# A decode block on one core: weight blocks cut by rows instead of by columns, with partial sums added outside PSUM and a new order of the late loads

## The chip, the cores and the metric

The kernel runs on one core of a Trainium2 chip. The metric is the device time of one execution in microseconds, as the median of several runs, lower being better. A ratio is the mean time of one kernel's runs over that of the kernel before in the same rounds on the same chip. It is therefore not quite the ratio of the medians that are quoted beside it.

A profile is one execution. Its span, from first to last instruction, is about 2 us shorter than the time. Positions "at 360 us" are counted from the start of the span.

## The reference, cut to what matters

One token per sequence, for 8 sequences, goes through a modulated attention and a modulated gated MLP. All tensors are bf16.

```
mod = silu(c) @ w_mod                              # w_mod 1024 x 6144
h = layernorm(x) * (1 + ca) + sa
q = h @ wq                                         # wq 1024 x 4096, 32 heads of 128
o = softmax(q @ k_cache^T / sqrt(128)) @ v_cache   # each cache 8 x 4 x 8192 x 128
x = x + ga * (o @ wo)                              # wo 4096 x 1024
h = layernorm(x) * (1 + cb) + sb
x = x + gb * ((relu(h @ W_gate) * (h @ W_up)) @ W_down)   # 1024 x 3584, 3584 x 1024
```

Each cache has 8 sequences x 4 heads x 8192 positions x 128, and a head of the cache serves 8 query heads. One sequence's head is 2 MB, so the 64 of K and V are 134 MB. The weights are 51 MB. Each byte is used once, so the work is to move 186 MB into the core.

## The kernel before: the parts that matter

Weights travel in blocks of up to 2 MB into slots of SBUF. There are four weight slots (`wslot`), four for K (`ksl`), three for V (`vsl`) and one scratch area (`scr`) that serves the MLP at the end. SP issues the weight and K loads in one fixed order, and waits in that order. ACT issues the V loads. Blocks of w_mod, wq, gate and up are cut by columns:

```python
for jb in range(6):
    wblocks.append(("mod", jb, w_mod[:, 1024 * jb:1024 * (jb + 1)].rearrange("(kc p) n -> p kc n", p=128), KC, 1024))
...
def dense_T(i, act_T, col_of_fb, nfb, key_last=None):
    pe_wait_wblock(i)
    ...
    for fb in range(nfb):
        for kc in range(KC):               # all 8 parts of the contraction are in the block
            pe.op(... e.matmul(T.X_ps[:, col:col + B], wv[:, kc, 128 * fb:128 * (fb + 1)], act_T[:, kc, :],
                               start=(kc == 0), stop=(kc == KC - 1)), ...)
```

A partition then receives eight pieces of 1,024 columns, 2,048 bytes each (1,024 bytes in the last, narrower block of gate and up). K and V give each partition one piece of 16,384 bytes. A slot is loaded again when its last reader is done. For the late weights the rule is:

```python
if region in region_last:      free = ("pe", ("wdone", region_last[region]))
elif region[0] == "w":         free = None
elif region[0] == "k":         free = ("pe", ("sdone", last_k_user[region[1]]))   # scores 28..31
elif region[0] == "v":         free = ("pe", ("pvdone", last_v_user[region[1]]))
else:                          free = ("pe", ("pvdone", B * G - 1))
```

On PE, a batch's four score products come first, and the products with V of the batch before come around the softmax steps (cut):

```python
for b in range(B):
    st_phase(b)                                 # 4 K tiles: scores
    if b >= 1: pv_pairs(b - 1, [0, 1])          # 2 V tiles of the batch before
    softmax_pe_1(b)
    if b >= 1: pv_pairs(b - 1, [2, 3])
    softmax_pe_2(b)
pv_pairs(B - 1, [0, 1]); pv_pairs(B - 1, [2, 3])
```

Then follow wo, the second norm, gate/up and down. Down's blocks go into the weight slots that wo leaves. K31 and V31 below are the last K and V tiles (counted from 0).

## Time and profile before

| | kernel before |
|---|---|
| time | 457.57 us median of 4 (457.41 to 458.21) |
| span | 455.6 us |
| bytes | 186.4 MB, mean 409 GB/s |
| PE / DVE / ACT busy | 40% / 20% / 5% |
| chain that ended last | DMA 82% |

The next fence has lines of the page: the DMA engines' mean busy share in tenths in 40 slices of the span, what they moved, packets by size, SP's load queue q1 (packets, MB, share of the 16 engines) and the chain that ended last.

```profile
...
DMA  7999999999999999999999999999999999999992
GB/s 293 443 402 408 407 407 424 432 405 424 433 434 419 432 430 433 426 429 426 434 427 427 431 432 421 430 434 429 424 432 433 416 431 421 412 365 382 379 405 94
DMA packets 35838, 186.40 MB, mean 409 GB/s; under 512 B 1464, under 2 KB 3512, under 8 KB 27600
...
q1 hardware_dynamic: 31184, 118.54, 64.1%
...
DMA 82%; PE 11%; SPq 3%; DVE 2%; issue 2%; ACT 0%
```

The DMA row is full from the second slice to the last but one, so time is bytes over rate. The rate is not the same everywhere. The windows view shows it: each line has a stretch, its length, busy time and count of PE, weight loads, DVE, ACT and GpSimd, the granted PE clock, the DMA share and GB/s.

```profile
34.00:68.00 34.00, 13.37 (x456) 12.79 (x456) 1.30 (x5) 0.00 (x0) 0.00 (x0) 1.00 1.05 408
250.00:300.00 50.00, 19.64 (x589) 17.78 (x588) 15.96 (x13) 3.82 (x2) 0.00 (x0) 1.00 1.01 430
360.00:370.00 10.00, 5.89 (x194) 5.38 (x194) 2.44 (x2) 0.00 (x0) 0.00 (x0) 1.00 1.01 413
400.00:420.00 20.00, 10.85 (x288) 9.31 (x284) 5.44 (x11) 0.20 (x1) 0.00 (x0) 0.95 1.01 368
```

With 16,384-byte packets (250 to 300 us) it is 430 GB/s. With 2,048-byte packets (34 to 68 us) it is 408, though the engines are no less busy. In the MLP's loads (400 to 420 us) it is only 368. Single packets in the trace took a median of 611 ns for 16,384 bytes, 84 for 2,048 and 46 for 1,024.

### The profile page before, as it was taken

The numbers are of one execution on the slowest core, as the hardware profiler recorded it, in microseconds if no ns is written. First come the engines' busy times: TensorE is split into PE (matmuls) and PEld (weight loads), VectorE is DVE, ScalarE is ACT, GpSimd is POOL, SyncE is SP. The second block draws the span as 40 slices with busy tenths as digits, with TensorE's granted clock in tenths as the row PEclk, the third lists the DMA queues.
The fourth block names the chain that finished last, engine by engine and source line by source line (L and its number), as shares of the span: only waits on it lengthen the run. The fifth ranks groups of instructions, "written<-read, shape, count | busy, mean of one in ns | idle before, by whom it ended". The sixth has DMA issues, their size and how long they took to land.

```text
span 455.6 us, 11881 instructions
## 1 busy us (share of the span) xinstructions
PE 183.4 (40%) x5784; PEld 170.3 (37%) x5784; DVE 90.4 (20%) x101; ACT 22.6 (5%) x17; POOL 1.3 (0%) x9
## 2 busy tenths in 40 slices
PE   2013431340362652354175245317524544373853
PEld 2013431330362652353164235316414543372853
DVE  4000100025025025004302500420250033004001
ACT  3000001001001001001000100100010011000000
POOL 1000000000000000000000000000000000000000
PEclk9999999999999999999999999999999999998555
DMA  7999999999999999999999999999999999999992
GB/s 293 443 402 408 407 407 424 432 405 424 433 434 419 432 430 433 426 429 426 434 427 427 431 432 421 430 434 429 424 432 433 416 431 421 412 365 382 379 405 94
DMA packets 35838, 186.40 MB, mean 409 GB/s; under 512 B 1464, under 2 KB 3512, under 8 KB 27600
## 3 DMA queue, kind: packets, MB, share of 16 engines
q1 hardware_dynamic: 31184, 118.54, 64.1%
q10 hardware_dynamic: 4608, 67.11, 34.6%
q8 instruction: 45, 0.74, 0.6%
q14 instruction: 1, 0.01, 0.0%
HBM read 185.63 MB, written 0.02 MB: 407 GB/s over the span
## 4 chain that ended last, share of the span: by engine, by line
DMA 82%; PE 11%; SPq 3%; DVE 2%; issue 2%; ACT 0%
DMA ksl<-in_A_k_cache_dram 60%; DMA wslot<-in_w_mod_dram 7%; DMA vsl<-in_A_v_cache_dram 7%; DMA wslot<-in_A_wq_dram 4%; DMA wslot<-in_B_W_down_dram 4%; PE S_ps L495 3%; SPq L61 3%; PE X_ps L477 3%; PE X_ps L578 2%; PE OT_ps L512 2%; PE S_ps L467 1%; DVE mpart L392 1%; DVE xc L348 0%; DVE stat L343 0%; DVE S_ps L351 0%
## 5 line engine op out<-in xcount | busy, mean ns | idle before, releaser
L512 PE MATMUL OT_ps<-scr,vsl 128*128 128x8 bf16 x2048 | 59.5, 168 | 105.7 <-DMA vsl<-in_A_v_cache_dram 105.4
L512 PEld LDWEIGHTS OT_ps<-scr,vsl 128*128 128x128 bf16 x2048 | 57.0, 104 | 107.9 <-DMA vsl<-in_A_v_cache_dram 107.4
L495 PE MATMUL S_ps<-qT,ksl 128*128 128x8 bf16 x2048 | 58.6, 168 | 66.3 <-DMA ksl<-in_A_k_cache_dram 53.6
L495 PEld LDWEIGHTS S_ps<-qT,ksl 128*128 128x128 bf16 x2048 | 56.6, 104 | 68.2 <-DMA ksl<-in_A_k_cache_dram 41.9
L392 DVE TENSOR_REDUCE mpart<-S_ps 128x32 f32<-128x2048 f32 x8 | 18.3, 2292 | 142.2 <-PE S_ps L495 142.2
L409 DVE TENSOR_REDUCE lpart<-scr 128x32 f32<-128x2048 bf16 x8 | 28.6, 3571 | 15.8 <-ACT scr L319 15.8
L319 ACT ACTIVATE scr<-scr 128x2048 bf16<-128x2048 f32 x8 | 15.3, 1909 | 285.6 <-DVE scr L404 285.6
L477 PE MATMUL X_ps<-siluT,wslot 128*128 128x8 bf16 x384 | 11.2, 168 | 35.8 <-DMA wslot<-in_w_mod_dram 35.8
L477 PEld LDWEIGHTS X_ps<-siluT,wslot 128*128 128x128 bf16 x384 | 10.7, 104 | 36.3 <-DMA wslot<-in_w_mod_dram 32.2
L404 DVE TENSOR_TENSOR scr<-S_ps,nb 128x2048 f32<-128x2048 f32 x8 | 18.3, 2291 | 0.3
L412 DVE RECIPROCAL rrow<-X_ps 1x32 f32<-1x32 f32 x8 | 2.8, 346 | 58.7 <-PE X_ps L529 58.7
L477 PE MATMUL X_ps<-hT,wslot 128*128 128x8 bf16 x256 | 7.5, 168 | 12.7 <-DMA wslot<-in_A_wq_dram 12.7
L477 PEld LDWEIGHTS X_ps<-hT,wslot 128*128 128x128 bf16 x256 | 7.2, 104 | 13.1 <-DMA wslot<-in_A_wq_dram 10.0
L379 DVE COPY modT<-X_ps 128x384 f32<-128x384 f32 x1 | 0.6, 557 | 42.3 <-PE X_ps L477 42.3
L578 PE MATMUL X_ps<-ot_sb,wslot 128*128 128x8 bf16 x256 | 7.3, 168 | 3.7 <-issue 3.0
L578 PEld LDWEIGHTS X_ps<-ot_sb,wslot 128*128 128x128 bf16 x256 | 7.1, 104 | 3.9 <-issue 3.1
L477 PE MATMUL X_ps<-h2T,ksl 128*128 128x8 bf16 x256 | 7.1, 168 | 2.2 <-issue 1.6
L477 PEld LDWEIGHTS X_ps<-h2T,ksl 128*128 128x128 bf16 x256 | 7.0, 104 | 2.4 <-issue 1.7
L524 PEld LDWEIGHTS X_ps<-diag,ones 32*128 32x128 f32 x16 | 3.9, 304 | 8.7 <-DVE diag L397 8.7
L524 PE MATMUL X_ps<-diag,ones 32*128 32x32 f32 x16 | 5.0, 405 | 5.1 <-DVE diag L397 5.1
L521 PE MATMUL X_ps<-identf,mpart 128*32 128x128 f32 x16 | 5.1, 420 | 4.8 <-DVE mpart L392 2.4
L395 DVE TENSOR_REDUCE negm<-X_ps 32x1 f32<-32x128 f32 x8 | 2.2, 279 | 22.9 <-PE X_ps L521 22.9
(73 smaller groups left out, 75.5 us busy)
## 6 DMA issues: line engine op xcount, KB each, us to landing
vsl<-in_A_v_cache_dram ACTq DMA_DIRECT2D x32, 2048.0 KB, 24.0
ksl<-in_A_k_cache_dram SPq DMA_DIRECT2D x32, 2048.0 KB, 27.2
wslot<-in_w_mod_dram SPq DMA_DIRECT2D x6, 2048.0 KB, 24.0
wslot<-in_A_wq_dram SPq DMA_DIRECT2D x4, 2048.0 KB, 18.7
wslot<-in_A_wo_dram SPq DMA_DIRECT2D x4, 2048.0 KB, 26.1
wslot<-in_B_W_down_dram SPq DMA_DIRECT2D x3, 2048.0 KB, 17.9
ksl<-in_B_W_gate_dram SPq DMA_DIRECT2D x2, 2048.0 KB, 48.7
ksl<-in_B_W_up_dram SPq DMA_DIRECT2D x2, 2048.0 KB, 35.0
```

The lines of the kernel that those rows point to most:

```text
L61: self.e.dma_start(out_ap, in_ap).then_inc(self.K.dsem[sem_name], 16)
L319: act.op(lambda e: e.activation(T.pt[:, b % 2, 0:NCOL], T.ssub[:, 0:NCOL], ACT.Exp), key=("exp", b))
L392: dve.op(lambda e: e.tensor_reduce(T.mpart[:, :], T.S_ps[:, 0:NCOL].rearrange("p (c j) -> p j c", c=NCX), AX.X, ALU.max), key=("mpart", b))
L404: dve.op(lambda e: e.tensor_tensor(out=T.ssub[:, 0:NCOL].rearrange("p (c j) -> p c j", c=NCX), in0=T.S_ps[:, 0:NCOL].rearrange("p (c j) -> ...
L409: dve.op(lambda e, b=b: e.tensor_reduce(T.lpart[:, :], T.pt[:, b % 2, 0:NCOL].rearrange("p (c j) -> p j c", c=NCX), AX.X, ALU.add), key=(" ...
L467: pe.op(lambda e, fb=fb: e.matmul(T.S_ps[0:B, 128 * fb:128 * (fb + 1)], srcT[:, fb * B:fb * B + B], T.identf[:, :], start=True, stop=True) ...
L477: pe.op(lambda e, fb=fb, kc=kc, col=col, wv=wv: e.matmul(T.X_ps[:, col:col + B], wv[:, kc, 128 * fb:128 * (fb + 1)], act_T[:, kc, :], star ...
L495: pe.op(lambda e, b=b, p=p, kv=kv, cix=cix, col=col: e.matmul(T.S_ps[:, col:col + REP], kv[:, cix, :], T.qT[:, b, REP * p:REP * (p + 1)], ...
L512: pe.op(lambda e, p=p, cix=cix, col=col, vv=vv, ptv=ptv: e.matmul(T.OT_ps[:, col:col + REP], vv[:, cix, :], ptv[:, cix, REP * p:REP * (p + ...
L521: pe.op(lambda e: e.matmul(T.X_ps[0:32, 0:128], T.mpart[:, 0:32], T.identf[:, :], start=True, stop=True), key=("P1", b))
L524: pe.op(lambda e: e.matmul(T.X_ps[:, 128:160], T.ones[0:32, 0:128], T.diag[0:32, 0:32], start=True, stop=True), key=("P2", b))
L578: pe.op(lambda e, fb=fb, hq=hq, wvs=wvs: e.matmul(T.X_ps[:, fb * B:fb * B + B], wvs[hq // 8][:, hq % 8, 128 * fb:128 * (fb + 1)], T.ot_sb[ ...
```

## The change

The intent is larger packets. Blocks of w_mod, wq, gate and up are cut by rows of the weight, so that a partition's piece is a whole row: 12,288, 8,192 and 7,168 bytes. Such a block holds only a part of the contraction, and PSUM no longer sums over blocks. DVE adds each block's partial result to an accumulator in SBUF, and two PSUM banks take turns. To find room, several small buffers share memory. The order of the late loads changes too: wo's four blocks wait for batches 0 to 3, and the K slots go to gate/up only after the third-last product with V ("the gate" below). The core of the diff:

```diff
-    for jb in range(6):
-        wblocks.append(("mod", jb, w_mod[:, 1024 * jb:1024 * (jb + 1)].rearrange("(kc p) n -> p kc n", p=128), KC, 1024))
+    for kc in range(KC):
+        wblocks.append(("mod", kc, [(lambda r: r[:, 0:6 * D], w_mod[128 * kc:128 * (kc + 1), :])]))
 ... (wq: two row groups a block; gate and up: one row group of each a block)
     for i in load_order:
         region = assign[i]
-        if region in region_last:
+        if region in region_last and region_last[region] >= n_phaseA:
             free = ("pe", ("wdone", region_last[region]))
         elif region[0] == "w":
-            free = None
+            free = ("pe", ("sdone", min(B * G - 1, _wj[0] * G + G - 1)))
+            _wj[0] += 1
         elif region[0] == "k":
-            free = ("pe", ("sdone", last_k_user[region[1]]))
+            free = ("pe", ("pvdone", B * G - 3))
 ...
+            for kc in range(KC):
+                dve.wait("pe", ("modpart", kc))
+                pb = PB[kc % 2]
+                if kc == 0:
+                    dve.op(... e.tensor_copy(modflat, pb[:, 0:48 * B]) ...)
+                else:
+                    dve.wait_self()
+                    dve.op(... e.tensor_tensor(out=modflat, in0=pb[:, 0:48 * B], in1=modflat, op=ALU.add) ...)
 ... (the same for q in 4 and gate/up in 8 parts; PE waits for the add of two blocks ago before it writes a bank)
```

## The prediction

> **What bounds the kernel now: the DMA engines.** In the page's 40 slices the DMA row reads 9 in 38 of them; the chain of waits is 82% DMA. PE is busy 40%, DVE 20%. 186.4 MB move at a mean of 409 GB/s. Where only K and V move (16,384-byte packets) the windows view gives 428 to 430 GB/s; from 34 to 68 us, where only w_mod, wq and wo move (2,048-byte packets), it gives 407 to 408; from 400 to 440 us (gate/up/down, 1,024 and 2,048-byte packets) only 359 to 396.
>
> Packets in the trace take median 0.611 us for 16,384 bytes, 0.084 for 2,048, 0.046 for 1,024. Corrected for the overlap of neighbouring packets (DMA share 1.01 and 1.05) this fits about 5.6 ns fixed plus 36.6 ps per byte on one engine. The Trainium skill, "DMA: Bandwidth & Descriptors", section "Why small descriptors are slow (HBM only)", names a fixed overhead per packet (about 3 cycles); the trace agrees in kind.
>
> **What the change does.** w_mod, wq, gate and up (35.7 MB) are cut by rows, so their packets grow from 2,048/1,024 to 12,288, 8,192 and 7,168 bytes: 18,432 packets become about 4,096. wo and down stay at 2,048. Bytes and matmuls stay. Partial sums over kc move from PSUM accumulation to DVE adds: 18 small adds or copies of 128x256 to 128x448; the 128x384 copy took 0.56 us, so about 10 us of DVE, hidden under block loads of about 4 us each; one last add per stage (0.6 us) is exposed to the chain at most. The wo loads are spread over batches 0 to 3, and gate/up loads into the K slots wait for the third-last V product.
>
> **Cost, as estimates from those durations.** 14,300 fewer packets x 5.6 ns / 16 engines = 5.0 us (cross-check: 35.7 MB at 408 instead of 429 GB/s is 4.3 us). All on the DMA path: about 2.6 us before attention, 2 us after. In the tail the trace also shows starved slices (402 to 404, 408 to 413, 426 to 433 us, at 250 to 350 GB/s), together about 2.9 us of bandwidth, where SP's issues last 4 to 6 us each. Gate/up with fewer, larger packets should remove over half of that. Against it: when K's last load lands, nothing but V25/V26 is queued; V27 is issued only about 4 us later, and the gate loads that used to fill in no longer do: a hole of about 1 us. The end of the chain after the last down block (5.6 us) and the 4 to 5 us in which the DMA engines drain unevenly stay. Attention stays at about 39 us a batch.
>
> Sum: about -4.5 -2 +1 = -5.5 us. Predicted: 452.0 us, range 447.5 to 455; faster by over 2% 0.15, within 2% 0.82, slower by over 2% 0.03.
>
> **What would show it right:** packets under 8 KB from 27,600 to about 11,200; slices before attention at 425 to 430 GB/s; first K batch complete 8 to 13 us earlier because wo no longer goes first; attention slope unchanged; wo still at about 407; tail slices at 420 or more while gate/up load; the chain still ending in a wait for down.
>
> **What would make it wrong:** a hole over 3 us where gate/up loads now start; 7,168-byte packets slower than the fit; a tail bound by PE (about 50 us after the last V); large packets removing the uneven drain, which would give over 2%.

## The result, and the profile after

| | before | changed |
|---|---|---|
| time, median | 457.65 us (12 runs, 457.22 to 458.38) | 453.53 us (9 runs, 453.06 to 454.70) |
| ratio | | 0.9909 (95% interval 0.9898 to 0.9919) |
| span | 455.6 us | 451.2 us |

The change gains 0.9%, which is inside the 2% band. The prediction was 452.0 with a range of 447.5 to 455. The same lines of the changed kernel's page:

```profile
...
DMA  7999999999999999999999999999999989999993
GB/s 309 428 431 428 424 431 430 428 422 424 428 428 425 426 426 429 421 431 430 426 417 432 433 424 430 431 430 428 428 427 431 399 338 428 420 424 425 415 406 129
DMA packets 21662, 186.40 MB, mean 413 GB/s; under 512 B 1624, under 2 KB 1624, under 8 KB 11376
...
q1 hardware_dynamic: 17008, 118.54, 62.7%
...
DMA 81%; PE 12%; DVE 3%; issue 2%; SPq 1%; ACT 0%
```

and the same windows of it:

```profile
34.00:68.00 34.00, 11.66 (x392) 11.08 (x392) 4.25 (x11) 0.00 (x0) 0.00 (x0) 1.00 1.01 427
250.00:300.00 50.00, 22.57 (x702) 20.77 (x699) 17.89 (x14) 3.82 (x2) 0.00 (x0) 1.00 1.01 430
360.00:370.00 10.00, 7.08 (x214) 6.37 (x210) 4.39 (x5) 0.00 (x0) 0.00 (x0) 1.00 0.87 331
400.00:420.00 20.00, 10.68 (x265) 8.82 (x265) 6.20 (x13) 0.20 (x1) 0.00 (x0) 1.00 1.02 425
```

SP's queue has 17,008 packets for the same 118.54 MB instead of 31,184. The stretch of w_mod and wq runs at 427 GB/s instead of 408 and that of gate/up at 425 instead of 368 (in the changed kernel V2's load overlaps the first until 39.9 us; w_mod alone, from 41 to 48 us, moves at 424 against 406 before). The K/V stretch is unchanged. One thing is worse: from 360 to 370 us the rate falls to 331 (413 before). That is the hole that the gate opens between the last K and the first gate/up load.

How the end hangs together is seen in the chain of waits in order of time (start, duration, what), here from the last V on:

```profile
379.66 14.20 DMA vsl<-in_A_v_cache_dram
393.90 1.88 PE OT_ps L525 x64
...
427.05 1.49 PE OT_ps L634 x56
...
429.69 15.99 DMA wslot<-in_B_W_down_dram
445.73 1.03 PE OT_ps L651 x32
...
```

V31 lands at 393.9 us. PE and DVE need until about 428.7 for its product (L525), wo, the norm and gate/up (L634). Then PE waits, and the last block of down lands at 445.7; from there to the end of the span are 5.5 us. So two clocks run at the end: "last landing + 5.5 us", and "last V + the work that hangs on it". Here the first ends later. The chain of the kernel before ends in the same wait:

```profile
...
383.68 14.81 DMA vsl<-in_A_v_cache_dram
...
433.08 16.98 DMA wslot<-in_B_W_down_dram
...
450.10 1.03 PE OT_ps L607 x32
...
```

Comparing landings in the two traces, the last K came at 361.5 before and 358.5 after (3.0 us gained), the last V at 398.5 and 393.9 (4.6), the last block of down at 450.1 and 445.7 (4.4).

### The profile page after: what moved, and what is told of

Its sections match the earlier page's. It is cut to its first block, busy times and chain, and to the rows that moved or that the text cites. A ratio compares the mean times of both kernels' runs of the same rounds, so it can differ in the third digit from the quotient of the medians.

```text
span 451.2 us, 11940 instructions
## 1 busy us (share of the span) xinstructions
PE 184.1 (41%) x5784; PEld 170.6 (38%) x5784; DVE 100.9 (22%) x120; ACT 22.5 (5%) x16; POOL 1.3 (0%) x9
## 3 DMA queue, kind: packets, MB, share of 16 engines
q1 hardware_dynamic: 17008, 118.54, 62.7%
## 4 chain that ended last, share of the span: by engine, by line
DMA 81%; PE 12%; DVE 3%; issue 2%; SPq 1%; ACT 0%
DMA ksl<-in_A_k_cache_dram 48%; DMA vsl<-in_A_v_cache_dram 20%; DMA wslot<-in_w_mod_dram 10%; DMA wslot<-in_B_W_down_dram 4%; PE OT_ps L525 3%; PE S_ps L508 2%; PE X_ps L612 2%; PE X_ps L634 1%; PE OT_ps L634 1%; PE S_ps L494 1%; DVE guacc L427 1%; SPq L61 1%; PE OT_ps L569 1%; DVE scr L422 1%; ACT scr L324 0%
## 5 line engine op out<-in xcount | busy, mean ns | idle before, releaser
L525 PE MATMUL OT_ps<-scr,vsl 128*128 128x8 bf16 x2048 | 60.0, 168 | 86.0 <-DMA vsl<-in_A_v_cache_dram 81.5
L525 PEld LDWEIGHTS OT_ps<-scr,vsl 128*128 128x128 bf16 x2048 | 57.2, 104 | 88.3 <-DMA vsl<-in_A_v_cache_dram 83.1
L410 DVE TENSOR_REDUCE guacc<-S_ps 128x32 f32<-128x2048 f32 x8 | 18.3, 2292 | 141.5 <-PE S_ps L508 141.5
L427 DVE TENSOR_REDUCE guacc<-scr 128x32 f32<-128x2048 bf16 x8 | 28.5, 3568 | 15.8 <-ACT scr L324 15.8
L422 DVE TENSOR_TENSOR scr<-S_ps,guacc 128x2048 f32<-128x2048 f32 x8 | 18.3, 2291 | 0.3
L569 PE MATMUL X_ps<-siluT,wslot 128*128 128x8 bf16 x192 | 5.7, 168 | 17.5 <-DMA wslot<-in_w_mod_dram 17.5
L569 PE MATMUL OT_ps<-siluT,wslot 128*128 128x8 bf16 x192 | 5.8, 168 | 16.0 <-DMA wslot<-in_w_mod_dram 16.0
L569 PEld LDWEIGHTS X_ps<-siluT,wslot 128*128 128x128 bf16 x192 | 5.4, 104 | 17.8 <-DMA wslot<-in_w_mod_dram 15.2
L569 PEld LDWEIGHTS OT_ps<-siluT,wslot 128*128 128x128 bf16 x192 | 5.4, 104 | 16.4 <-DMA wslot<-in_w_mod_dram 16.4
L537 PEld LDWEIGHTS X_ps<-guacc,ones 32*128 32x128 f32 x16 | 4.0, 304 | 8.7 <-DVE guacc L415 8.7
L537 PE MATMUL X_ps<-guacc,ones 32*128 32x32 f32 x16 | 5.0, 405 | 5.1 <-DVE guacc L415 5.1
L545 PE MATMUL X_ps<-guacc,ones 1*128 1x32 f32 x16 | 5.0, 407 | 3.5 <-DVE guacc L430 3.5
```

Source lines behind the costliest of these rows:

```text
L410: dve.op(lambda e: e.tensor_reduce(T.mpart[:, :], T.S_ps[:, 0:NCOL].rearrange("p (c j) -> p j c", c=NCX), AX.X, ALU.max), key=("mpart", b))
L422: dve.op(lambda e: e.tensor_tensor(out=T.ssub[:, 0:NCOL].rearrange("p (c j) -> p c j", c=NCX), in0=T.S_ps[:, 0:NCOL].rearrange("p (c j) -> ...
L427: dve.op(lambda e, b=b: e.tensor_reduce(T.lpart[:, :], T.pt[:, b % 2, 0:NCOL].rearrange("p (c j) -> p j c", c=NCX), AX.X, ALU.add), key=(" ...
L525: pe.op(lambda e, p=p, cix=cix, col=col, vv=vv, ptv=ptv: e.matmul(T.OT_ps[:, col:col + REP], vv[:, cix, :], ptv[:, cix, REP * p:REP * (p + ...
L537: pe.op(lambda e: e.matmul(T.X_ps[:, 128:160], T.ones[0:32, 0:128], T.diag[0:32, 0:32], start=True, stop=True), key=("P2", b))
L545: pe.op(lambda e: e.matmul(T.X_ps[:, 192:224], T.ones[0:1, 0:128], T.rrow[0:1, 0:32], start=True, stop=True), key=("P4", b))
```

## The experiments

The theory: the gain is the fixed cost of packets that no longer exist, and the hole gives a part of it back. Rivals: the new order of the loads is what gains; DMA time goes by bytes alone; the adds cost on the chain; the gate is what makes large packets pay. All kernels below gave correct results and were run four times each. Landings are those of the one profiled run, in us from the start of its span.

| run | kernel | time us | ratio to before | last V | last down |
|---|---|---|---|---|---|
| (before) | | 457.65 | 1 | 398.5 | 450.1 |
| (changed) | | 453.53 | 0.9909 | 393.9 | 445.7 |
| e1 | changed, no gate | 459.45 | 1.0036 | 405.5 | 445.6 |
| e2 | before + both orders | 457.25 | 0.9989 | 395.9 | 450.7 |
| e3 | changed, w_mod in 1,024 B | 457.09 | 0.9982 | 397.8 | 449.7 |
| e4 | changed, DVE steps doubled | 453.60 | 0.9911 | 393.6 | 445.6 |
| e5 | before + wo spread | 457.09 | 0.9978 | 398.5 | 449.6 |
| e6 | changed, one block ungated | 454.62 | 0.9927 | 398.7 | 445.6 |
| e7 | changed, down in 16,384 B | 457.37 | 0.9975 | 395.1 | 446.1 |
| e8 | changed, one V product earlier | 453.47 | 0.9912 | 393.9 | 445.7 |
| e9 | e8, gate opens earlier | 454.07 | 0.9921 | 396.6 | 445.8 |
| e10 | changed, w_mod in 2,048 B | 455.27 | 0.9946 | 396.7 | 448.6 |
| e11 | changed, scores issued three times | 490.65 | 1.0714 | 432.6 | 484.4 |
| e12 | changed, 2,560 idle waits on GpSimd | 453.92 | 0.9914 | 394.9 | 446.8 |

### e3 and e10: is it the packets?

w_mod's rows are laid into SBUF with gaps, so that a row can't be one packet. Blocks, bytes, order and the rows read from HBM stay as in the changed kernel. e3, with 512 columns a piece (e10: 1,024 columns, pitch 1,280):

```diff
-("mod", kc, [(lambda r: r[:, 0:6 * D], w_mod[128 * kc:128 * (kc + 1), :])])
+("mod", kc, [(lambda r: r[:, 0:7680].rearrange("p (j n) -> p j n", n=640)[:, :, 0:512],
+              w_mod[128 * kc:128 * (kc + 1), :].rearrange("p (j n) -> p j n", n=512))])
```

> The changed kernel with w_mod's rows laid out with gaps in SBUF, so that its packets are 1,024 bytes instead of 12,288 (12,288 packets instead of 1,024); same bytes, same blocks, same order. Theory (5.6 ns fixed per packet and engine): 11,264 x 5.6 ns / 16 = 3.9 us more, about 457.4. Rival (DMA time goes by bytes; the packets' size is a by-product): within 0.7 us of 453.5. If the cost per packet grows for small ones, more than 5 us.

> A second dose of e3: w_mod in packets of 2,048 bytes (6,144 instead of 1,024) in the changed kernel. e3 gave 3.5 us for 11,264 more packets, 5.0 ns per packet and engine; the same cost here gives 5,120 x 5.0 ns / 16 = 1.6 us more, about 455.1. If the cost sets in only below 2,048 bytes: under 0.7 us.

The page's packet line, first e3:

```profile
DMA packets 32926, 186.40 MB, mean 409 GB/s; under 512 B 1624, under 2 KB 13912, under 8 KB 23664
```

then e10:

```profile
DMA packets 26782, 186.40 MB, mean 410 GB/s; under 512 B 1624, under 2 KB 1624, under 8 KB 17520
```

With 11,264 packets more, e3 took 3.6 us more (3.5 against e4 in the same rounds), where 3.9 was expected; with 5,120 more, e10 took 1.7 us more, where 1.6 was expected. Over 16 engines that is 5.0 and 5.4 ns for each packet on one engine. The rival "bytes alone" is out. Since the rows read are as contiguous as in the changed kernel, it is the packets and not the contiguity in HBM that count.

Another rival is that SP issues such loads more slowly (its eight issues for w_mod last 41.6 us in all in e3, 31.0 in e10 and 3.3 in the changed kernel) and so leaves engines without work. In the first 5 us that may play a part: e3 and e10 moved 108 and 97 GB/s there, the changed kernel 171, which is 0.7 and 0.9 us at full rate. Later it does not: from 41 to 48 us, where w_mod alone loads, the rates are 384, 406 and 424 GB/s, with the engines never less busy in e3 and e10 (DMA share 1.09, 1.05 and 0.99). For all of w_mod's 12.58 MB these rates make 4.4 and 4.1 ns per packet, so a part of the 5 ns may be the later start.

### e2, e5 and e1: packet size against gate

e2 gives the kernel before both new orders; e5 gives it the wo order alone; e1 takes the gate from the changed kernel. Each edit is the lines of the diff above, applied or undone, for instance e1:

```diff
         elif region[0] == "k":
-            free = ("pe", ("pvdone", B * G - 3))
+            free = ("pe", ("sdone", last_k_user[region[1]]))
```

> The kernel before with everything of the change's load order but none of its packets: wo spread over batches 0 to 3, and K slots given to gate/up only after the third-last V product. Theory (the gain is packets alone): no gain; the hole costs, so 457.6 plus 2 to 3 us, about 460. Rival (the order of the loads is what gains): 453 to 456 us.

> The kernel before with the spread of the wo loads alone (small packets, K slots free after their last score). With e1 (large packets, the same freeing), e2 (small, gated) and the changed kernel (large, gated) it makes a square of packet size by gate. Theory (wo's order is worth nothing; small packets take little from V, about a tenth beside 16,384-byte packets, so the gate matters only for large ones): 457.6 plus or minus 0.7 us, last V at about 396 to 399 us, starved stretches after 400 us as before. Rival (wo's spread is a gain that e2 hid under the gate's hole): 454 to 456 us.

> The changed kernel with one undo: a K slot is given to gate/up as soon as its last K was used (scores 28 to 31), as before the change, instead of after the third-last V product. Theory (the change gains by larger packets and gives about 3 us back in a hole that the gate opens): the hole at 360 to 372 us (331 GB/s) closes, 420 GB/s or more there, time about 450.5 us against 453.5, that is 2 to 3 us less. Rival (the gate protects V, and releasing gate/up early takes bandwidth from V and so delays the chain V, wo, norm, gate/up): the last V lands 2 us or more later than 393.9 and the time is 453.5 or more.

wo is spread in all four corners of this square:

| | K slots free after their last score | gated |
|---|---|---|
| small packets | 457.09 (e5) | 457.25 (e2) |
| large packets | 459.45 (e1) | 453.53 (changed) |

Both of my expectations about the gate fell. For small packets it costs nothing clear of noise, though its hole is there, and I had expected 2 to 3 us. (wo's order alone, e5, is worth about 0.2%: 0.9978, interval 0.9963 to 0.9993.) For large packets it is worth 5.9 us, and I had expected its removal to gain; the rival written down for e1, that the gate protects V, is what came.

First e1. The window of the hole shows that it was filled:

```profile
360.00:370.00 10.00, 5.96 (x165) 5.12 (x161) 3.38 (x5) 0.00 (x0) 0.00 (x0) 1.00 1.00 421
```

and its chain shows what that did:

```profile
386.51 19.00 DMA vsl<-in_A_v_cache_dram
...
405.56 1.88 PE OT_ps L525 x64
...
439.93 2.71 issue
...
446.80 1.87 PE X_ps L651 x64
...
```

V31 landed at 405.5 instead of 393.9. The chain no longer has a wait for down: it goes without DMA from V's product to down's (L651). All of down had landed at 445.6, and the end came only at 457.4. The work after the last V took 51.9 us (457.4 - 405.5) and it set the end. (In the changed kernel the same work would end at 393.9 + 51.9 = 445.8 us, 5.4 us before its span's end.) The prediction had named this as what could make it wrong.

Why did V suffer so much more from large packets? (With small ones the gate moves V31 from 398.5 to 395.9 us, with large ones from 405.5 to 393.9.) The Trainium skill, "DMA: Bandwidth & Descriptors", section "Queues, rings and completion order", says that an engine takes turns between the queues at the granularity of packets. The trace agrees that the turns are about even: between 377 and 392 us, e1's engines started 272 packets of gate/up and 274 of V. In e5 there were 381 and 336. (A packet of the trace is one piece of a row; the page's packet is a group of some 9 to 17 descriptors. The counts show how even the turns are, not how long one is.) When turns are about even, bandwidth goes by packet size. Gate/up took 1.95 of 6.44 MB (30%) with 7,168-byte packets, and 0.78 of 6.29 MB (12%) with 2,048-byte ones. Making the weights' packets larger thus made the weights a stronger rival to V, and the gate keeps them apart.

Now e2. In the same window its hole is as deep as the changed kernel's:

```profile
360.00:370.00 10.00, 5.50 (x193) 5.37 (x194) 2.29 (x1) 0.00 (x0) 0.00 (x0) 1.00 0.78 313
400.00:420.00 20.00, 10.27 (x251) 8.43 (x248) 5.57 (x12) 0.20 (x1) 0.00 (x0) 1.00 1.06 403
```

But from 400 to 420 us it runs at 403 GB/s with the same small packets that gave 368 before. In e5, which has the same packets and the same order of wo but no gate, it is the other way round:

```profile
360.00:370.00 10.00, 6.07 (x194) 5.54 (x194) 2.29 (x1) 0.00 (x0) 0.00 (x0) 1.00 1.04 425
400.00:420.00 20.00, 11.28 (x288) 9.43 (x285) 5.07 (x9) 0.18 (x1) 0.00 (x0) 0.99 1.00 366
```

So the hole and the low rate of the old tail, which the prediction counted as two terms, trade against each other. The landings say how. Each load raises its semaphore, the counter that its readers wait for, in 16 steps, and the trace has 16 DMA engines; I take each step as the landing of one engine's part. These are the times of the 16 parts after the first of them:

```
before,  V25 (last part at 364.6): 0.0 0.2 0.2 0.2 0.3 0.4 0.4 1.2   6.0 6.1 6.1 6.1 6.2 6.3 6.6 7.3
changed, V25 (last part at 362.3): 0.0 0.0 0.1 0.3 0.4 0.6 0.7 1.0   5.8 5.8 5.9 5.9 6.0 6.2 6.2 7.3
changed, V28 (last part at 377.4): 0.0 0.0 0.2 0.4 0.8 0.9 0.9 1.0   1.1 1.1 1.3 1.4 1.4 2.2 2.2 2.4
```

During attention eight parts come to trail the other eight by some 6 us. A load counts as landed when its last part has. In the hole of the changed kernel the early engines run dry while the late ones still have work: V25 to V30 land at 362.3, 367.1, 372.4, 377.4, 382.3 and 387.1, about 5 us apart, which is the time of 2 MB at full rate. The late engines never stop, and the hole costs those that were ahead. A count of the packets that are under way at once bears this out. From 360.5 to 363 us the changed kernel has 8 or 9, half of the usual 16, and after 363.7 never under 13 until 440 us. e2 has 7 to 9 from 363 to 365.8 us and never under 15 from 400 to 440. The kernel before and e5 have never under 15 from 355 to 400 us, and fall to 9 or 10 in short stretches after 400. So it is half of the engines that stand still, in the hole with the gate and in the tail without it. That they are the same ones from load to load is an inference, since the trace does not name the engine of a packet.

### e6, e8 and e9: is the hole worth filling?

e6 releases only the first gate/up block early (region 0 of the K slots as in e1, the rest gated). e8 leaves the loads alone and moves one product of PE, so that V24's slot is free earlier:

```diff
-                st_phase(b)
+                last_b = (b == B - 1)
+                st_phase(b, (lambda: pv_pairs(B - 2, [0])) if last_b else None)   # called before the last K's scores
                 if b >= 1:
-                    pv_pairs(b - 1, [0, 1])
+                    pv_pairs(b - 1, [1] if last_b else [0, 1])
```

e9 is e8 with the gate at `B * G - 4`.

> The changed kernel with only the first gate/up block (1.8 MB, 4.3 us of transfer) let into its K slot as soon as that slot's last score is done; the other blocks stay gated. If the hole at 360 to 372 us is time that any load could use: 2 to 3 us less than 453.5, last V delayed by under 2 us. If the hole is only where engines that run ahead wait for those that lag (paid once, here or at the end): within 0.8 us of 453.5, with the last V 2 to 4 us later. If V's chain is what ends last after all: more than 454.5.

> The changed kernel with one product moved in PE's order: in the last batch the product with V24 comes before the last K's scores instead of after them, so V24's slot is free, and V27 is asked for, some 5 us earlier (357 instead of 362 us). Nothing is added ahead of V on the DMA. If the hole at 360 to 372 us comes from V27 and V28 being asked for late: the hole shrinks to under 1 us, the last V lands 2 to 4 us before 393.9, and the time falls 2 to 3 us, to about 451. If the hole is only engines that run ahead waiting for those that lag: under 0.7 us of change.

> As e8, and the gate of gate/up opens one V product earlier (the fourth-last). If a stretch of idle DMA remains in e8 while softmax of the last batch runs: up to 1 us less than e8. If gate/up then shares with the last V loads and V's chain is near the bound: 0 to 2 us more than e8.

e6 took 454.62 us, with V31 4.8 us later (398.7), so that the work after V set the end again (452.8 - 398.7 = 54.1 us), while the last landing stayed at 445.6. e8 took 453.47 us, no change, with V31 at 393.9; its window at 360 to 370 us:

```profile
360.00:370.00 10.00, 6.60 (x192) 5.83 (x189) 4.72 (x5) 0.00 (x0) 0.00 (x0) 1.00 0.90 351
```

The hole did not close: the next request still had to wait for V25's late parts. e9 took 454.07, 0.6 more than e8, with intervals that overlap (0.9903 to 0.9940, 0.9894 to 0.9930). In e1, e4, e6, e8 and e9 the last landing is within 445.6 and 445.8 us, hole or no hole. With small packets throughout (before, e2, e5) it is 449.6 to 450.7. For e8 this is the outcome that was expected if the hole is only engines ahead waiting for those behind. e6's last landing says the same, while its time was set by the other clock.

### e4: do the adds cost?

Ahead of each partial sum's add stands a copy of the same bank (two copies of 224 columns for gate/up). That makes 28 further steps, not the 20 that the expectation says, and 12.2 us more of DVE. For instance:

```diff
                 pb = PB[kc % 2]
+                dve.wait_self()
+                dve.op(lambda e, pb=pb: e.tensor_copy(T.guacc[:, 0:48 * B], pb[:, 0:48 * B]))
                 if kc == 0:
```

> The changed kernel with a further DVE copy of each partial-sum bank ahead of its add (20 more steps on 128x224 to 128x384, about 10 us more DVE work). Theory (the adds hide under the block loads, and behind the K loads where they end a stage): under 0.7 us more. Rival (they sit on the chain): each block's add delays the next block, 5 us or more.

It took 453.60 us against 453.53. In the window from 34 to 68 us DVE was busy for 7.66 us instead of 4.25, and the rate stayed:

```profile
34.00:68.00 34.00, 11.65 (x392) 11.07 (x392) 7.66 (x18) 0.00 (x0) 0.00 (x0) 1.00 1.01 428
```

The adds are hidden, as predicted. One 128x384 add takes 558 ns, while a block of w_mod takes 3.7 us at 428 GB/s (1.57 MB).

### e7: the last small packets

Down's rows are dealt to the partitions eight in a row, so that a partition's piece is 16,384 bytes. To match, PE takes gate/up's columns with a step of 8 (4 in the last group):

```diff
-B_W_down[r0:r0 + rr, :].rearrange("(kk p) n -> p kk n", p=128)
+B_W_down[r0:r0 + rr, :].rearrange("(p kk) n -> p kk n", p=128)
-reg[:, wbase + 128 * fb:wbase + 128 * (fb + 1)],
+reg[:, wbase + r0:wbase + r0 + rr].rearrange("p (q k) -> p k q", k=nk)[:, fb % 8, :],    # r0, rr, nk of group fb // 8
```

> The changed kernel with down's rows dealt to the partitions eight in a row, so that its packets are 16,384 bytes (8,192 in the last block) instead of 2,048; the columns of gate/up are taken with a step of 8 (4) to match. Theory (the last landing is DMA-bound, 5 ns per packet and engine): 3,136 packets fewer, about 1.0 us less than 453.5, with up to 2 us more if SP's long issues of 1,024 descriptors were starving engines. Rival (the end of the chain is not DMA, or strided weight loads slow PE): 453.5 or more; PE's gate/up matmuls longer than 1.5 us per 56 would show it.

It took 457.37 us, 3.8 more. The chain names the cause, 56 matmuls of gate/up at a time (compare L634 in the changed kernel, 1.49 us):

```profile
...
424.97 3.16 PE X_ps L639 x56
428.13 3.16 PE OT_ps L639 x56
...
```

and so do the groups of instructions, where a weight load with the step takes 163 ns and one without 104 (the mean ns of one stands after the busy time):

```profile
L639 PEld LDWEIGHTS OT_ps<-hT,ksl 128*128 128x128 bf16 x112 | 6.5, 163 | 0.0
...
L617 PEld LDWEIGHTS X_ps<-ot_sb,wslot 128*128 128x128 bf16 x172 | 4.8, 104 | 3.4 <-issue 3.4
```

The Trainium skill, "SBUF — State Buffer", in a note in the section on the DMA port swizzle, says that SBUF has lines of 16 bytes and that reads want at least two hits per line. A step of 8 bf16 values is one value per line, and the slower load agrees with that. The rate during down's loads was higher (430 to 440 us: 428 GB/s against 407), but the last landing was not earlier (446.1). By the semaphore's steps, 15 of the last block's 16 parts were there at 444.8, 0.9 us before the changed kernel's fifteenth (445.7), which is near the 1.0 us expected; the sixteenth came 1.3 us after them. Why that one was late is open.

### e11 and e12: who are the late engines?

I suspected the instruction fetches, 45 packets of 16,384 bytes in a queue of their own (q8). e11 issues each score matmul of batches 2 to 6 three times; e12 puts 2,560 waits on an already reached semaphore value behind GpSimd's setup.

> The changed kernel with each score matmul of batches 2 to 6 issued three times (2,560 further PE instructions, the same result): no load is added, but more instructions are fetched by DMA. In the landings of each load's 16 parts, 8 always come early and 8 late, by 2 to 7 us, and the late ones fall behind in steps near 0.6 to 0.9 us. If the late 8 are those that carry the instruction fetches (45 packets of 16,384 bytes now): about 10 more such packets, 10 x 0.61 to 0.93 / 8 = 0.8 to 1.2 us later last landing (445.6 to about 446.6), and time about 454.5. If the lag has another cause: last landing within 0.3 us of 445.7. If the PE work itself delays the loads of K: over 2 us more, and DMA share below 1 before 355 us.

> e11 was no test of the lag: PE's own work held up the K loads. Here the further 2,560 instructions are waits on an already reached semaphore value on GpSimd, which has nothing else to do after its setup; no engine that works is touched. If the 8 late engines are late through instruction fetches: some 10 to 20 more packets in the instruction queue (45 now), the late parts of the last landing fall back by 0.6 to 1.2 us or more (last landing 446.3 to 447.5 against 445.7), and the time grows by as much. If the lag has another cause: last landing within 0.3 us of 445.7. If no further packets show in the instruction queue, the run tells nothing about it.

e11 was no test. PE's own work held back the K loads, the time rose to 490.65 us, and the DMA row shows gaps inside attention:

```profile
DMA  8999999999999999969997999599949969999993
...
q8 instruction: 65, 1.06, 0.8%
```

e12's further instructions came through another queue, in packets of 8,192 bytes:

```profile
q8 instruction: 45, 0.74, 0.6%
q14 instruction: 11, 0.09, 0.0%
```

Its profiled run has the last landing 1.1 us later (446.8), but the time, 453.92, has a ratio of 0.9914 with an interval of 0.9897 to 0.9930, which covers the changed kernel's 0.9909. Nothing is shown either way. What makes eight engines late stays open.

No experiment beat the changed kernel clear of noise.

## Why the prediction was right, point by point

- **The bound was DMA before and after.** The chain's DMA share was 82% and is 81%, and it still ends in a wait for down. Right.
- **Packets.** Predicted were 5.0 us from 14,300 packets at 5.6 ns. The dosed runs gave 5.0 and 5.4 ns per packet with the later start, and 4.1 to 4.4 ns from the rates of w_mod alone, which makes 3.7 to 3.9 us. Swapping small for large packets under the same orders (e2 to e4, same rounds; e4 is worth the changed kernel) gave 3.7. The predicted size was about a third too large. The Trainium skill, "DMA: Bandwidth & Descriptors", section "Why small descriptors are slow (HBM only)", has the mechanism in kind, a fixed cost per packet. Its size here is what e3 and e10 measured.
- **Where it is gained.** Predicted 2.6 us before attention: the last K landed 3.0 us earlier, and 0.6 of that came with the new orders alone (360.9 us in e2 and e5), so 2.4 with the packets. The first batch's K was complete at 88.5 us instead of 96.2, that is 7.7 us, just under the predicted 8 to 13; with the new orders alone (e2, e5) it was complete at 90.7 us, so 5.5 us of it is the wo block that no longer goes first, and 2.2 us the packets. That wo itself still runs at about 407 could not be read: it never had the engines to itself.
- **Starved slices, -2 us, and the hole, +1 us.** This is the mis-sized part of the sum. The low rate of the tail did go (368 to 425 GB/s), and the hole came out deeper than predicted: from 360 to 380 us, at 331 and 405 instead of 429 GB/s, it lacks 1.2 MB, or 2.8 us of bandwidth. But e2 changed both at once with small packets and the time did not move clear of noise (0.9989, interval 0.9973 to 1.0006). The two terms are one: eight engines run ahead of eight, and the ones ahead wait either in the hole or in the tail. Their sum is about 0 instead of -1. The prediction did not have this mechanism, so it is luck that its sum of the two came within 1 us. With the packets' 0.8 less (3.7 for the 4.5 of the sum), that makes about -3.7, and -4.1 was measured, where -5.5 was predicted.
- **DVE adds.** Hidden, as predicted (e4).
- **The gate.** The prediction listed it as a cost only. It costs nothing clear of noise, and it protects 5.9 us (e1). The prediction's clause of a tail bound by PE, "about 50 us after the last V", was the right warning: e1 measured 51.9.

## What to carry to other kernels

When DMA is the bound, the estimate "packets removed x fixed cost / 16 engines" came out a third too high here, with the fixed cost read from the medians of three packet sizes in the trace; the rate of a stretch in which such packets load alone was the better source. Larger packets also take a larger share of the engines beside another queue, so a prefetch that was harmless with small packets can delay the loads on which the chain hangs; gate it behind them. An idle stretch in the DMA row is not time to be had before it is clear that the engines which finish last were idle too.

## What the Trainium skill lacked or had wrong

- "DMA: Bandwidth & Descriptors", Specifications, gives 512 bytes as the least transfer for line rate. Here, with w_mod alone loading from 41 to 48 us, 1,024-byte packets moved at 384 GB/s (e3), 2,048-byte ones at 406 (e10) and 12,288-byte ones at 424 (changed).
- Same page, "Why small descriptors are slow (HBM only)": it calls the joining of consecutive descriptors into packets worth it only at 256 bytes or less. It does not say what larger descriptors are worth above that. Here going from 2,048 to 12,288 bytes was worth 1.7 us for 12.6 MB (e10), 4.1 to 5.4 ns per packet and engine.
- Same page, "Where 436 GB/s comes from": for HBM to SBUF the HBM side, about 358 GB/s, is said to bind. The sentence lacks the condition that the page's table of measurements has beside it, that both cores of a pair stream: this one core read HBM at 430 GB/s through 250 to 300 us.
- Same page, "Queues, rings and completion order": the turns by packet are there, the consequence is not. Two loaded queues shared about in the ratio of their packet sizes (30% for gate/up in 7,168-byte packets and 12% in 2,048-byte ones, both beside 16,384-byte packets).
- No page says that of a load's 16 parts eight can trail the other eight by 6 to 7 us after 350 us of streaming, so that an average DMA share below 1 need not delay any landing.
- "DMA: Bandwidth & Descriptors", "Queues, rings and completion order": row 14 is listed for "refill", with no other row for instructions. If the trace's queue numbers are these rows, GpSimd's further instructions showed there (1 packet to 11, e12), but PE's showed in q8 (45 to 65, e11).
- "SBUF — State Buffer", the note on 16-byte lines: it also lists a step of 8 bf16 as free. A weight load with that step took 163 ns instead of 104 (e7).
